# The carried state's products in four 64x64 quadrants of TensorE, with the state as the stationary operand and the outputs in two banks

## The chip, the core and the metric

The kernel runs on one core of a Trainium2 chip. Its engines are PE (TensorE, matrix products into PSUM), DVE (VectorE), ACT (ScalarE), POOL (GpSimd) and SP (SyncE, which here only issues DMAs). PEld is the loading of PE's stationary operand. The metric is the device time of one execution in microseconds (us), as the median of several runs.

## What is computed

Two stages stand in a row. The first is a linear recurrence over time for 4 batches and 8 heads of width 48, the second a two-layer network on the tokens that it gives.

```python
for t in range(S):                                   # S = 768, r, k, v, w: (4, 8, 768, 48)
    cur = np.einsum('bhd,bhe->bhde', u[None] * kt, vt)
    y[:, :, t] = np.einsum('bhd,bhde->bhe', rt, state + cur)
    state = wt[:, :, :, None] * state + np.einsum('bhd,bhe->bhde', kt, vt)
x = y.transpose(0, 2, 1, 3).reshape(B * S, H * D)    # 3072 tokens of 384
h = x @ w_in                                         # 384 x 2048
g = np.maximum(h, 0.0) + alpha * np.minimum(h, 0.0)
out = g @ w_out                                      # 2048 x 384
```

## The kernel before

**Attention.** The 768 steps are cut into 6 chunks of 128, so that with 4 batches there are 24 units q = 0 to 23 (chunk c = q // 4, batch b = q % 4). For each q, `load` brings in decays, k and r with the head's width on the partitions (`wd`, `kr`), and v (`nv`). `prep` makes running products of the decays with two scans on DVE (L367, L373) and scales k and r with them (L376, L379). `scores` (L430) multiplies k by r into two PSUM banks, DVE writes the part before the diagonal over ACT's diagonal (L435, tile `at`). `outputs` then adds three things on PE. For c > 0 the carried state acts on the scaled r (L526). The new part of the state is the transposed k times v (L479). The scores times v (L472) complete the output. Two heads lie above each other on the 128 partitions, head 2p in rows 0 to 63 and head 2p + 1 in rows 64 to 127, each 48 wide.

**The carried state.** `St[b]` holds the state of a batch, 128 x 4 x 48. `carry` scales it on POOL (L415), and ACT copies its two halves into the diagonal blocks of `Sd`, 128 x 4 x 128 with zeros elsewhere (L419, two copies). L526 then runs four products of the whole 128x128 array, one for each pair of heads. The output tile `yp` is one PSUM bank, and the new state goes to another, `up`.

**Split outputs.** The network runs in fp32r on a high and a low part of each number. `take` copies `yp` in two pieces (384 and 128 columns) to the high part on ACT (L492). The low part is the difference, on DVE (L503) from q = 6 on, before that by a product with minus the identity on PE (L497) and ACT (L501).

**Network.** Three q form a group g of 384 tokens, 8 groups in all. A step is one (g, j) with j one of 16 slices of the hidden width: 9 products L605, activation on ACT and DVE (L610, L612), the split into `gh` and `gl` (L614, L615), and two steps later 9 products L624. The weights of slice j are unpacked once from 8-byte numbers by ACT and DVE; the last of these steps is `wl` (L591, 17 instructions in all). The first three groups run j = 0 to 5 first, then j = 6 to 15, so step 28 is the first that needs the last weight slice.

**Order.** Nothing runs in the order of the code. Each piece is recorded with `op(engine, duration, function, reads, writes, due)`, and `Plan.order` places all pieces by a simulated clock with these durations, due times and free buffers. The order on each engine is what that plan gives. PSUM has three banks for the network's results and a ring of five, `bank`, for all else.

Of the kernel before, what the change touches and what calls it, by code (L numbers as in the profile page):

```python
# [20 lines left out]
P = 128  # L21
# [29 lines left out]
MODES = {("M", "R"): 0.2, ("R", "M"): 0.2, ("M", "C"): 0.1, ("C", "M"): 0.15, ("C", "R"): 0.1, ("R", "C"): 0.1}  # L51
# [162 lines left out]
def fast_path(tc, wgt, flag, dmaj, nat, u, wts, alpha, out, part):  # L214
# [12 lines left out]
    with tc.tile_pool(name="const", bufs=1) as const, tc.tile_pool(name="psum", bufs=1, space=PSUM) as psum:  # L227
# [10 lines left out]

        Sd = const.tile([P, NP, P], F32, name="Sd")
# [11 lines left out]
        St = [const.tile([P, NP, D], F32, name=f"St{b}") for b in range(B)]  # L251
# [39 lines left out]
        for o in range(2):  # L291
            op("SP", 0.4, lambda o=o: nc.sync.dma_start(
                out=u_dm[ROWS[o], :, o:o + 1], in_=u.rearrange("(p o d) -> o d p", o=2, d=D)[o].unsqueeze(2)),
               w=[("u_dm", o)], lat=0.05)
# [17 lines left out]
        op("POOL", 0.6, lambda: nc.gpsimd.memset(Sd, 0.0), w=[("Sd", 0), ("Sd", 1)])  # L312
# [44 lines left out]
        def prep(q):  # L357
# [37 lines left out]
            else:  # L395
                for i in range(2):
# [4 lines left out]
                    out=cd.ap.rearrange("p (o a) -> p a o", o=2),  # L401
                    in_=rk.ap[:, 0:HD].rearrange("p (a o d) -> p a o d", o=2, d=D), axis=AX.X, op=ALU.add), r=[rk], w=[cd])
# [52 lines left out]
        def outputs(q, nxt):  # L455


            c, b = divmod(q, B)
# [6 lines left out]
            yp = Tensor(bank)  # L465
            up = Tensor(bank) if c < NC - 1 else None
            dst = slice(0, KT)

            def pair(p, start, stop):
                for o in range(2):  # L470
                    h = 2 * p + o
                    nc.tensor.matmul(yp.ap[FULL[o], p * P:(p + 1) * P], lhsT=nv.ap[:, h * 64:(h + 1) * 64],  # L472
                                     rhs=at.ap[:, o, p, :], start=start, stop=stop)

            def state():
                for p in range(NP):
                    for o in range(2):
                        h = 2 * p + o
                        nc.tensor.matmul(up.ap[FULL[o], p * D:(p + 1) * D], lhsT=kn[:, p, FULL[o]],  # L479
                                         rhs=nv.ap[:, h * 64:h * 64 + D], start=True, stop=True)  # L480

            def take(last):


                parts = [(0, lambda i: x.ap[:, i, :, ss], x, 0.45)]
                if last:
                    parts.append((KT * P, lambda i: xr.ap[:, i, ss], xr, 0.25))

                def src(c0):
                    return pairs(yp.ap[:, 0:KT * P], P) if c0 == 0 else yp.ap[:, c0:]  # L490
                for c0, dst, key, t in parts:
                    op("ACT", t, lambda c0=c0, dst=dst: nc.scalar.copy(out=dst(0), in_=src(c0)), r=[yp], w=[(key, (s, 0))])  # L492
                if q < LO_BY_PE:

                    def rests():
                        for c0, dst, key, t in parts:
                            nc.tensor.matmul(src(c0), lhsT=minus, rhs=dst(0), start=False, stop=True, skip_group_check=True)  # L497
                    op("PE", 0.25 * len(parts), rests, r=["minus", *[(key, (s, 0)) for _, _, key, _ in parts]], w=[yp], kind="MM")
                for c0, dst, key, t in parts:
# [442 lines left out]
```

## Time and profile before

| | us |
|---|---|
| median of 3 runs | 541.84 (541.06 to 547.21) |
| profiled execution | 540.92 |
| its span, first to last instruction | 539.1 |
| PE busy in the span | 518.3 (96%) |
| DVE busy | 348.4 (65%) |
| ACT busy | 324.2 (60%) |
| POOL busy | 56.9 (11%) |

The profiled execution's own time lies 1.8 us over its span and 0.9 us under the median. An engine's busy share is an average over the span; the stages differ, and they are read one by one below. In rows, the name before `<-` is what an instruction writes, the names behind it are what it reads. A float32 product of the code shows as two PE records, an fp32r product as one.

### The profile page before, as it was taken

The page shows a single profiled execution, that of the slowest core. Times are in us where ns is not written, and L with a number is a line of the kernel's source. Part 1 is how long each engine was busy: PE and PEld are TensorE (multiplying, and loading weights), DVE is VectorE, ACT ScalarE, POOL GpSimd, SP SyncE. Part 2 cuts the span into 40 slices and gives each one's busy share as a digit, 9 for nine tenths or more (in the row PEclk, how much of TensorE's full clock was granted, in tenths as well). Part 3 has the DMA queues.
Part 4 walks back from the last instruction along what each step waited for, and adds up shares of the span by engine and source line. Part 5 has one row for each costly group of instructions (what it writes and reads, how often), then busy time and mean ns, then how long its engine had stood idle before and what let it go on. Part 6 is the DMA issues. An engine that isn't in the chain of part 4 may idle for free.

```text
span 539.1 us, 9763 instructions
## 1 busy us (share of the span) xinstructions
PE 518.3 (96%) x3733; PEld 501.0 (93%) x3733; DVE 348.4 (65%) x595; ACT 324.2 (60%) x802; POOL 56.9 (11%) x74
## 2 busy tenths in 40 slices
PE   5997989999999999999999999999999999999995
PEld 5877878989999999999999999999999999999995
DVE  5799999999995738665736566556474444333332
ACT  2677777765654346555646567668777675653332
POOL 2000514240000201210100110110000000000000
PEclk9599989999999999999999999999999999999999
DMA  8357677754623206544507344546354243021001
GB/s 303 126 179 253 249 219 255 247 170 144 191 72 102 96 12 215 160 129 142 157 28 202 115 164 127 158 169 223 120 190 141 66 155 118 11 74 42 0 2 50
DMA packets 29655, 75.14 MB, mean 139 GB/s; under 512 B 4064, under 2 KB 10912, under 8 KB 29600
## 3 DMA queue, kind: packets, MB, share of 16 engines
q1 hardware_dynamic: 29600, 74.44, 42.6%
q8 instruction: 31, 0.51, 0.4%
q14 instruction: 24, 0.20, 0.1%
HBM read 65.87 MB, written 6.49 MB: 134 GB/s over the span
## 4 chain that ended last, share of the span: by engine, by line
PE 74%; DVE 14%; DMA 5%; issue 3%; ACT 2%; SPq 1%; DVEq 0%; ACTq 0%
PE bank L605 30%; PE op L624 30%; PE bank L430 4%; DMA raw<-in_wts_dram 4%; PE bank L472 3%; PE bank L526 3%; DVE gl L615 2%; DVE raw L586 2%; DVE wd L373 2%; DVE wl L591 1%; PE bank L479 1%; DMA u_dm<-in_u_dram 1%; DVE cx L583 1%; DVE at L435 1%; PE bank L390 1%
## 5 line engine op out<-in xcount | busy, mean ns | idle before, releaser
L605 PE MATMUL bank<-x,wh 128*128 128x384 f32 x768 | 218.9, 339 | 3.2 <-ACT kn L451 1.8
L605 PEld LDWEIGHTS bank<-x,wh 128*128 128x128 f32 x768 | 140.5, 188 | 6.2 <-ACT kn L451 2.1
L610 ACT ACTIVATE pos<-bank,alpha_n 128x384 f32<-128x384 f32 x128 | 74.1, 579 | 98.6 <-PE bank L605 97.5
L624 PE MATMUL op<-wh,gl 128*128 128x384 f32 x384 | 129.5, 337 | 3.3 <-DVE gl L615 3.3
L624 PE MATMUL op<-wh,gh 128*128 128x384 f32 x384 | 129.8, 338 | 0.0
L624 PE MATMUL op<-wl,gh 128*128 128x384 f32 x384 | 129.0, 336 | 0.0
L605 PE MATMUL bank<-x,wl 128*128 128x384 f32 x384 | 128.5, 335 | 0.2 <-DVE wl L591 0.2
L612 DVE SCALAR_TENSOR_TENSOR pos<-bank,pos 128x384 f32<-128x384 f32 x128 | 70.5, 551 | 80.5 <-ACT pos L610 80.1
L615 DVE TENSOR_TENSOR gl<-pos,gh 128x384 fp32r<-128x384 f32 x128 | 74.9, 585 | 52.1 <-ACT gh L614 51.9
L614 ACT CAST gh<-pos 128x384 fp32r<-128x384 f32 x128 | 65.4, 511 | 54.2 <-DVE pos L612 54.0
L624 PEld LDWEIGHTS op<-wh,gl 128*128 128x128 f32 x384 | 72.5, 189 | 4.9 <-DVE gl L615 4.8
L624 PEld LDWEIGHTS op<-wh,gh 128*128 128x128 f32 x384 | 72.4, 189 | 0.6
L605 PEld LDWEIGHTS bank<-x,wl 128*128 128x128 f32 x384 | 72.1, 188 | 0.5 <-DVE wl L591 0.5
L624 PEld LDWEIGHTS op<-wl,gh 128*128 128x128 f32 x384 | 72.5, 189 | 0.0
L406 ACT ACTIVATE at<-ident,cd 128x128 f32<-128x128 f32 x192 | 62.8, 392 | 0.9 <-PE bank L472 0.4
L435 DVE COPY_PREDICATED at<-mask,bank 128x512 f32<-128x512 int32 x48 | 33.1, 731 | 29.3 <-PE bank L430 26.7
L415 POOL TENSOR_TENSOR St<-St,pc_all 128x192 f32<-128x192 f32 x20 | 11.5, 577 | 260.1 <-ACT pc_all L382 253.0
L367 DVE TENSOR_TENSOR_SCAN suf<-wd,low 128x520 f32<-128x520 f32 x24 | 30.4, 1267 | 3.6 <-DMA wd<-in_dmaj_dram 3.6
L373 DVE TENSOR_TENSOR_SCAN wd<-wd,low 128x520 f32<-128x520 f32 x24 | 30.8, 1282 | 0.0
L430 PE MATMUL bank<-kr 64*128 64x128 f32 x384 | 29.7, 297 | 0.8 <-DVE kr L379 0.8
L430 PEld LDWEIGHTS bank<-kr 64*128 64x128 f32 x384 | 24.9, 199 | 4.9 <-issue 3.6
L397 POOL TENSOR_TENSOR rk<-rk,u_bc 128x384 f32<-128x384 f32 x18 | 20.2, 1120 | 78.2 <-DMA rk<-in_nat_dram 56.1
(84 smaller groups left out, 497.5 us busy)
## 6 DMA issues: line engine op xcount, KB each, us to landing
raw<-in_wts_dram SPq DMA_DIRECT2D x32, 768.0 KB, 4.6
kr<-in_dmaj_dram SPq DMA_DIRECT2D x24, 512.0 KB, 3.9
rk<-in_nat_dram SPq DMA_DIRECT2D x18, 384.0 KB, 3.5
wd<-in_dmaj_dram SPq DMA_DIRECT2D x24, 260.0 KB, 2.8
raw<-in_dmaj_dram SPq DMA_DIRECT2D x12, 520.0 KB, 4.3
nv<-in_nat_dram SPq DMA_DIRECT2D x24, 256.0 KB, 4.4
out_dram<-os SPq DMA_DIRECT2D x23, 192.0 KB, 1.9
x<-x3s SPq DMA_DIRECT2D x42, 48.0 KB, 2.2
```

The costliest lines, as they stand in the source:

```text
L367: op("DVE", 1.15, lambda: nc.vector.tensor_tensor_scan(out=suf.ap[:, ::-1], data0=w.ap[:, ::-1], data1=low[:, ::-1], initial=0.0, op0=ALU. ...
L373: op("DVE", 1.15, lambda: nc.vector.tensor_tensor_scan(out=w.ap, data0=w.ap, data1=low, initial=0.0, op0=ALU.mult, op1=ALU.max), r=["low"] ...
L397: op("POOL", 1.0, lambda i=i: nc.gpsimd.tensor_tensor(out=rk.ap[:, 0:HD], in0=rk.ap[:, 0:HD], in1=u_bc if i == 0 else rk.ap[:, HD:], op=AL ...
L406: nc.scalar.activation(out=at.ap[:, o, p, :], in_=ident, func=AF.Copy, scale=cd.ap[:, o * NP + p:o * NP + p + 1])
L430: nc.tensor.matmul(sps[o].ap[:, p * P:(p + 1) * P], lhsT=kr.ap[FULL[o], 0, p, :], rhs=kr.ap[FULL[o], 1, p, :], start=True, stop=True)
L435: op("DVE", 0.62, lambda o=o: nc.vector.copy_predicated(out=at.ap[:, o], mask=mask.unsqueeze(1).broadcast_to([P, NP, P]), data=pairs(sps[o ...
L605: nc.tensor.matmul(hp.ap[:, 0:GT], lhsT=a[:, j, 0, ks], rhs=x.ap[:, xi, k, :], start=(i == 0), stop=(i == 3 * KT - 1))
L610: op("ACT", 0.5, lambda: nc.scalar.activation(out=pos.ap, in_=hp.ap[:, 0:GT], func=AF.Relu, scale=alpha_n[:, j:j + 1]), r=[hp, "alpha"], w ...
L612: op("DVE", 0.55, lambda: nc.vector.scalar_tensor_tensor(out=pos.ap, in0=hp.ap[:, 0:GT], scalar=0.0, in1=pos.ap, op0=ALU.max, op1=ALU.subt ...
L614: op("ACT", 0.41, lambda: nc.scalar.copy(out=gh.ap, in_=pos.ap), r=[pos], w=[gh])
L615: op("DVE", 0.47, lambda: nc.vector.tensor_tensor(out=gl.ap, in0=pos.ap, in1=gh.ap.bitcast(F32), op=ALU.subtract), r=[pos, gh], w=[gl], lo ...
L624: nc.tensor.matmul(ops_[s], lhsT=a.ap[:, ts], rhs=w[:, j, 1, :], start=(j == j0 and i == 0), stop=(j == j1 - 1 and i == 2))
```

## The change

`Sd` is gone. `St[b]` becomes 128 x 4 x 64 with zeros in the last 16 columns, and is itself the stationary operand. Head p now lies in rows 0 to 63 and head 4 + p in rows 64 to 127, which the host's layout, `u` and the general path follow. Each of the four products of 128x128 becomes two of 64x64: the row half is that of the head (o), the column half is p % 2. So there are eight products in the four quadrants, and row half o writes to bank `yb[o]`. The scores times v go to the same two banks, and the new state to the free columns of `yb[0]`, so `up` is gone too. `take` now has three pieces: 256 columns of `yb[0]`, and twice 128 of `yb[1]`. The plan gets other durations and mode costs.

```diff
-MODES = {("M", "R"): 0.2, ...
+MODES = {("M", "Q"): 0.1, ("Q", "M"): 0.1, ("R", "Q"): 0.1, ("C", "Q"): 0.1, ("M", "R"): 0.2, ...
-        Sd = const.tile([P, NP, P], F32, name="Sd")
-        St = [const.tile([P, NP, D], F32, name=f"St{b}") for b in range(B)]
+        St = [const.tile([P, NP, 64], F32, name=f"St{b}") for b in range(B)]
-        op("POOL", 0.6, lambda: nc.gpsimd.memset(Sd, 0.0), w=[("Sd", 0), ("Sd", 1)])
+        for b in range(B):
+            op("POOL", 0.15, lambda b=b: nc.gpsimd.memset(St[b][:, :, D:], 0.0), w=[("St", b)])
...
                 op("POOL", 0.5, lambda: nc.gpsimd.tensor_tensor(
-                    out=St[b], in0=St[b], in1=pc_all[:, q, :].unsqueeze(2).broadcast_to([P, NP, D]), op=ALU.mult),
-                   r=[("pc", q)], w=[("St", b)], lock=True)
-                for o in range(2):
-                    op("ACT", 0.25, lambda o=o: nc.scalar.copy(out=Sd[FULL[o], :, 64 * o:64 * o + D], in_=St[b][FULL[o]]),
-                       r=[("St", b)], w=[("Sd", o)])
+                    out=St[b][:, :, 0:D], in0=St[b][:, :, 0:D], in1=pc_all[:, q, :].unsqueeze(2).broadcast_to([P, NP, D]),
+                    op=ALU.mult), r=[("pc", q)], w=[("St", b)], lock=True)
...
-            yp = Tensor(bank)
-            up = Tensor(bank) if c < NC - 1 else None
+            yb = Tensor(bank), Tensor(bank)
+            up = c < NC - 1
+            open_ = set()
+            def mm(o, rows, cols, stop=False, **kw):
+                nc.tensor.matmul(yb[o].ap[rows, cols], start=(o, rows.start) not in open_, stop=stop, skip_group_check=True, **kw)
+                open_.add((o, rows.start))
+            def pair(i, stop):
+                o = i // 2
+                for e in range(2):
+                    p = 2 * (i % 2) + e
+                    h = o * NP + p
+                    mm(o, FULL[e], slice((i % 2) * P, (i % 2 + 1) * P), stop, lhsT=nv.ap[:, h * 64:(h + 1) * 64], rhs=at.ap[:, o, p, :])
+            def carried(stop):
+                for p in range(NP):
+                    for o in range(2):
+                        mm(o, FULL[p % 2], slice(p // 2 * P, (p // 2 + 1) * P), stop and p > 1, lhsT=St[b][FULL[o], p, :],
+                           rhs=kr.ap[FULL[o], 1, p, :])
             def state():
                 for p in range(NP):
                     for o in range(2):
-                        h = 2 * p + o
-                        nc.tensor.matmul(up.ap[FULL[o], p * D:(p + 1) * D], lhsT=kn[:, p, FULL[o]],
-                                         rhs=nv.ap[:, h * 64:h * 64 + D], start=True, stop=True)
+                        h = o * NP + p
+                        mm(0, FULL[o], slice(2 * P + p * D, 2 * P + (p + 1) * D), lhsT=kn[:, p, FULL[o]],
+                           rhs=nv.ap[:, h * 64:h * 64 + D])
...
-                parts = [(0, lambda i: x.ap[:, i, :, ss], x, 0.45)]
+                parts = [(0, (0, 2), lambda i: x.ap[:, i, 0:2, ss], x, 0.35), (1, (0, 1), lambda i: x.ap[:, i, 2, ss], x, 0.25)]
                 if last:
-                    parts.append((KT * P, lambda i: xr.ap[:, i, ss], xr, 0.25))
+                    parts.append((1, (1, 2), lambda i: xr.ap[:, i, ss], xr, 0.25))
...
                 def products():
                     if c > 0:
-                        for p in range(NP):
-                            nc.tensor.matmul(yp.ap[:, p * P:(p + 1) * P], lhsT=Sd[:, p, :], rhs=kr.ap[:, 1, p, :],
-                                             start=(p == 0), stop=False)
+                        carried(False)
...
-                t = 1.28 + (0.97 if c > 0 else 0) + (0.42 if up else 0) + (1.0 if sc else 0)
+                t = 1.28 + (0.55 if c > 0 else 0) + (0.42 if up else 0) + (1.0 if sc else 0)
```

Two places of the new order matter. The first is PE's row around the carried products of q = 9. Before, they stand behind the 31st network step's L605 (`Sd` is the stationary operand, `nv` is v, `kn` the transposed k, `at` the scores, `op` the network's results):

```order
L624 MATMUL op_73<-wl,gh_125 128x384
L526 MATMUL bank_78<-kr_104,Sd 128x128 x4
L479 MATMUL bank_77<-nv_109,kn 64x48 x8
L472 MATMUL bank_78<-at_116,nv_109 64x128 x8
L430 MATMUL bank_76<-kr_105 128x128
```

In the changed kernel all products of `outputs` carry the helper's line L469, and this unit stands behind the 21st step's L605:

```order
L639 MATMUL op_74<-wl,gh_122 128x384
L469 MATMUL bank_78<-kr_103,St_93 64x128
L469 MATMUL bank_76<-kr_103,St_93 64x128
L469 MATMUL bank_78<-kr_103,St_93 64x128
L469 MATMUL bank_76<-kr_103,St_93 64x128
L469 MATMUL bank_78<-kr_103,St_93 64x128
L469 MATMUL bank_76<-kr_103,St_93 64x128
L469 MATMUL bank_78<-kr_103,St_93 64x128
L469 MATMUL bank_76<-kr_103,St_93 64x128
L469 MATMUL bank_78<-nv_108,kn 64x48 x8
L469 MATMUL bank_78<-at_115,nv_108 64x128 x4
L469 MATMUL bank_76<-at_115,nv_108 64x128 x4
```

Four products have become eight, which take the two banks in turn, and the whole unit has moved ten steps forward; the other units with c > 0 look the same (20 in all, 5 ahead of step 28 before and 6 now). Of those behind, q = 10, 14 and 15 stand six to eight steps earlier, the rest about where they stood.

The second place is DVE's row around the last weight slice, `wl`. Before, the scan L367 of the prep after next stands behind the last `wl`:

```order
L591 TENSOR_TENSOR wl<-raw_100,wh 128x768
L580 TENSOR_SCALAR cx_101<-raw_99 128x768
L615 TENSOR_TENSOR gl_126<-pos_121,gh_123 128x384
L583 SCALAR_TENSOR_TENSOR cx_101<-raw_99,cx_101 128x768
L612 SCALAR_TENSOR_TENSOR pos_122<-bank_76,pos_122 128x384
L586 ISA raw_99<-raw_99,cx_101 128x768x2
L615 TENSOR_TENSOR gl_127<-pos_122,gh_124 128x384
L373 SCALAR_TENSOR_TENSOR wd_103<-wd_103,low 128x520
L591 TENSOR_TENSOR wl<-raw_99,wh 128x768
L612 SCALAR_TENSOR_TENSOR pos_121<-bank_75,pos_121 128x384
L379 TENSOR_TENSOR kr_106<-kr_106,wd_103 128x512
L367 SCALAR_TENSOR_TENSOR suf_112<-wd_102,low 128x520
```

In the changed kernel (L379, L606 and L367 are the same pieces of work) the prep's L379 and the next prep's scan L367 stand ahead of the last `wl`:

```order
L379 TENSOR_TENSOR kr_105<-kr_105,wd_102 128x512
L627 SCALAR_TENSOR_TENSOR pos_120<-bank_79,pos_120 128x384
L606 TENSOR_TENSOR wl<-raw_98,wh 128x768
L598 SCALAR_TENSOR_TENSOR cx_100<-raw_99,cx_100 128x768
L630 TENSOR_TENSOR gl_125<-pos_120,gh_122 128x384
L601 ISA raw_99<-raw_99,cx_100 128x768x2
L627 SCALAR_TENSOR_TENSOR pos_121<-bank_75,pos_121 128x384
L367 SCALAR_TENSOR_TENSOR suf_111<-wd_101,low 128x520
L606 TENSOR_TENSOR wl<-raw_99,wh 128x768
```

Counted over DVE's whole row up to the last `wl`, the changed kernel has one L379, one L367 and four L435 more, one L615 fewer, and the low parts of q = 6 to 8 in nine pieces where there were six. Up to the same point PE's row (step 28) has two more units' scores, one more unit's transposes and outputs, and six L624 fewer.

## Rows read from the trace of the kernel before

**Rows 1.** The page: the span, the busy time of PE, DVE and ACT, and the span in 40 equal slices (busy share in tenths; PEclk is the granted TensorE clock in tenths).

```profile
span 539.1 us, 9763 instructions
PE 518.3 (96%) x3733; PEld 501.0 (93%) x3733; DVE 348.4 (65%) x595; ACT 324.2 (60%) x802; POOL 56.9 (11%) x74
...
PE   5997989999999999999999999999999999999995
...
PEclk9599989999999999999999999999999999999999
```

**Rows 2.** The windows by stage: length, then the busy time (and count) of PE, PEld, DVE, ACT and POOL, the granted clock, the DMA share and GB/s.

```profile
0.00:12.00 12.00, 5.87 (x29) 5.67 (x29) 7.95 (x11) 3.15 (x11) 2.91 (x18) 0.99 0.83 287
12.00:30.00 18.00, 17.75 (x150) 16.08 (x152) 12.50 (x22) 12.23 (x40) 0.00 (x0) 0.63 0.51 186
30.00:74.00 44.00, 37.88 (x342) 33.10 (x339) 43.76 (x66) 34.06 (x91) 8.58 (x7) 0.96 0.64 222
74.00:157.50 83.50, 81.24 (x573) 78.33 (x571) 81.22 (x131) 55.71 (x121) 19.70 (x19) 1.00 0.58 187
157.50:467.20 309.70, 309.40 (x2268) 302.29 (x2268) 178.38 (x321) 190.75 (x483) 25.67 (x30) 1.00 0.41 131
467.20:533.40 66.20, 66.13 (x382) 65.53 (x380) 24.55 (x48) 27.80 (x57) 0.00 (x0) 1.00 0.09 26
```

**Rows 3.** The windows of L526 alone (each product is two records).

```profile
30.00:157.50 127.50, 5.31 (x40) 5.11 (x40) 0.99 0.60 199
157.50:467.20 309.70, 15.78 (x120) 15.52 (x120) 1.00 0.41 131
```

**Rows 4.** The chain of waits around 157 us: start, length, what.

```profile
155.38 1.15 DVE wd L373
156.53 0.86 DVE wl L591
157.39 0.04 issue
157.44 1.68 PE bank L605 x8
```

**Rows 5.** PE's timeline around one unit with c > 0: start, length, line, shapes (stationary, then moving), count.

```profile
209.70 0.33 PE L624 MATMUL op<-wh,gl 128*128 128x384 f32 x1
209.87 0.34 PE L624 MATMUL op<-wl,gh 128*128 128x384 f32 x1
210.05 1.05 PE L526 MATMUL bank<-kr,Sd 128*128 128x128 f32 x8
211.03 0.67 PE L479 MATMUL bank<-nv,kn 128*64 128x48 f32 x16
211.53 1.06 PE L472 MATMUL bank<-at,nv 128*64 128x128 f32 x16
212.52 1.16 PE L430 MATMUL bank<-kr 64*128 64x128 f32 x16
213.62 0.44 PE L624 MATMUL op<-wh,gh 128*128 128x384 f32 x1
213.90 0.34 PE L624 MATMUL op<-wh,gl 128*128 128x384 f32 x1
214.07 0.34 PE L624 MATMUL op<-wl,gh 128*128 128x384 f32 x1
```

**Rows 6.** The same unit in narrow cuts of the timeline, each from another window: 211.04 to 211.05, 211.60 to 211.64, 211.64 to 211.70, 212.31 to 212.325 and 212.50 to 212.53. A row counts the records that run in its window.

```profile
210.83 0.28 PE L526 MATMUL bank<-kr,Sd 128*128 128x128 f32 x1
...
211.53 0.29 PE L472 MATMUL bank<-at,nv 128*64 128x128 f32 x2
...
211.53 0.41 PE L472 MATMUL bank<-at,nv 128*64 128x128 f32 x4
...
212.10 0.50 PE L472 MATMUL bank<-at,nv 128*64 128x128 f32 x6
...
212.31 0.28 PE L472 MATMUL bank<-at,nv 128*64 128x128 f32 x2
```

**Rows 7.** PE's timeline where a full-array product is followed by L430 alone, at 58 us.

```profile
58.22 0.34 PE L605 MATMUL bank<-x,wh 128*128 128x384 f32 x1
58.49 1.16 PE L430 MATMUL bank<-kr 64*128 64x128 f32 x16
59.58 0.45 PE L624 MATMUL op<-wh,gh 128*128 128x384 f32 x1
59.87 0.34 PE L624 MATMUL op<-wh,gl 128*128 128x384 f32 x1
```

**Rows 8.** Groups of instructions by line and shape: count, busy us, mean ns of one, and the idle time before them.

```profile
L435 DVE COPY_PREDICATED at<-mask,bank 128x512 f32<-128x512 int32 x48 | 33.1, 731 | 29.3 <-PE bank L430 26.7 <-ACT at L406 2.7
...
L367 DVE TENSOR_TENSOR_SCAN suf<-wd,low 128x520 f32<-128x520 f32 x24 | 30.4, 1267 | 3.6 <-DMA wd<-in_dmaj_dram 3.6
L379 DVE TENSOR_TENSOR kr<-kr,wd 128x512 f32<-128x512 f32 x24 | 16.4, 683 | 0.0
...
L503 DVE TENSOR_TENSOR x<-bank,x 128x384 fp32r<-128x384 f32 x18 | 9.8, 545 | 1.3 <-ACT x3s L492 1.3
...
L503 DVE TENSOR_TENSOR x3s<-bank,x3s 128x128 fp32r<-128x128 f32 x18 | 5.1, 281 | 0.0
```

**Rows 9.** The same view: the copies into `Sd`, and the high parts on ACT.

```profile
L419 ACT COPY Sd<-St 64x192 f32<-64x192 f32 x40 | 14.0, 349 | 2.2 <-PE bank L526 2.0
...
L492 ACT CAST x<-bank 128x384 fp32r<-128x384 f32 x24 | 11.3, 472 | 10.4 <-PE bank L472 10.4
...
L492 ACT CAST x3s<-bank 128x128 fp32r<-128x128 f32 x21 | 5.7, 269 | 0.0
```

**Rows 10.** PE's timeline where it starts again after a wait; in brackets the idle time and what ended it.

```profile
50.41 0.44 PE L605 MATMUL bank<-x,wh 128*128 128x384 f32 x1 [1.85 <-ACT kn L451]
...
70.02 0.69 PE L624 MATMUL op<-wh,gl 128*128 128x384 f32 x1 [1.35 <-DVE gl L615]
```

**Rows 11.** The windows around that second wait.

```profile
70.00:75.00 5.00, 4.99 (x21) 4.70 (x21) 4.89 (x9) 3.99 (x10) 0.74 (x2) 0.68 0.58 168
```

More of the change, by code (lines that the diff above doesn't have):

```diff
@@ L400, in prep @@
                 op("DVE", 0.47, lambda: nc.vector.tensor_reduce(
-                    out=cd.ap.rearrange("p (o a) -> p a o", o=2),
-                    in_=rk.ap[:, 0:HD].rearrange("p (a o d) -> p a o d", o=2, d=D), axis=AX.X, op=ALU.add), r=[rk], w=[cd])
+                    out=cd.ap, in_=pairs(rk.ap[:, 0:HD], D), axis=AX.X, op=ALU.add), r=[rk], w=[cd])
             for o, ps in ((o, range(i, i + 2)) for o in range(2) for i in (0, 2)):
@@ L486, in take, with src @@
                 if last:
-                    parts.append((KT * P, lambda i: xr.ap[:, i, ss], xr, 0.25))
[L489 to L492, printed above, removed]
+                    parts.append((1, (1, 2), lambda i: xr.ap[:, i, ss], xr, 0.25))
+                def src(o, i):
+                    return pairs(yb[0].ap[:, 0:2 * P], P) if o == 0 else yb[o].ap[:, i[0] * P:i[1] * P]
@@ L493, in take @@
+                for o, i, dst, key, t in parts:
+                    op("ACT", t, lambda o=o, i=i, dst=dst: nc.scalar.copy(out=dst(0), in_=src(o, i)), r=[yb[o]], w=[(key, (s, 0, o))])
                 if q < LO_BY_PE:
                     def rests():
-                        for c0, dst, key, t in parts:
-                            nc.tensor.matmul(src(c0), lhsT=minus, rhs=dst(0), start=False, stop=True, skip_group_check=True)
-                    op("PE", 0.25 * len(parts), rests, r=["minus", *[(key, (s, 0)) for _, _, key, _ in parts]], w=[yp], kind="MM")
@@ L499, in take @@
-                for c0, dst, key, t in parts:
+                        for o, i, dst, key, t in parts:
+                            nc.tensor.matmul(src(o, i), lhsT=minus, rhs=dst(0), start=False, stop=True, skip_group_check=True)
+                    op("PE", 0.2 * len(parts), rests, r=["minus", *[(key, (s, 0, o)) for o, _, _, key, _ in parts]], w=yb, kind="MM")
+                for o, i, dst, key, t in parts:
                     if q < LO_BY_PE:
-                        op("ACT", t, lambda c0=c0, dst=dst: nc.scalar.copy(out=dst(1), in_=src(c0)), r=[yp], w=[(key, (s, 1))])
+                        op("ACT", t, lambda o=o, i=i, dst=dst: nc.scalar.copy(out=dst(1), in_=src(o, i)), r=[yb[o]], w=[(key, (s, 1, o))])
@@ L513, in products @@
                 def products():
-                    for p in range(KT):
-                        nc.tensor.matmul(yp.ap[:, p * P:(p + 1) * P], lhsT=spread()[:, p, :], rhs=t3(s), start=(p == 0), stop=False)
-                    for p in range(KT):
-                        pair(p, False, p == KT - 1)
-                op("PE", 1.9, products, r=[sp, x3, (at, 0), (at, 1), nv], w=[yp], kind="MC", due=due_att[q] + 2.0)
-                op("PE", 0.5, state, r=["kn", nv], w=[up], kind="CC", due=due_att[q] + 10.0)
+                    for e in range(2):
+                        open_.discard((1, FULL[e].start))
@@ new lines, in products @@
+                    for i in range(KT):
+                        nc.tensor.matmul(yb[i // 2].ap[:, (i % 2) * P:(i % 2 + 1) * P], lhsT=spread()[:, i, :], rhs=t3(s),
+                                         start=(i % 2 == 0), stop=False, skip_group_check=True)
+                    open_.update((o, FULL[e].start) for o in range(2) for e in range(2))
+                    for i in range(KT):
+                        pair(i, i > 0)
+                op("PE", 1.9, products, r=[sp, x3, (at, 0), (at, 1), nv], w=yb, kind="MC", due=due_att[q] + 2.0)
```

69 lines of the change are left out of this document (34 added, 35 removed).

## The prediction

> **What bounds the kernel now.** I read the page first: PE is busy for 518.3 of 539.1 us, DVE for 348.4, ACT for 324.2, and after the first quarter PE's line shows full slices [rows 1]. Then I read the windows by stage [rows 2]. From 157.5 to 467.2 us PE is idle for 0.3 us, from there to 533.4 for 0.1. In this stretch whatever PE no longer does comes off the end, and what other engines do is free: DVE works for 178 of 310 us there, ACT for 191. Ahead of 157.5 us PE is idle for 6.1, 0.2, 6.1 and 2.3 us, and DVE is busy for 43.8 of 44.0 and 81.2 of 83.5 us. That front is ruled by both, and its last wait is PE's for the last weight slice: DVE ends a scan and `wl` at 157.39, PE goes on at 157.44 [rows 4]. The end is therefore T, the moment at which the last weight slice is unpacked, plus all PE work that the order leaves behind it.
>
> **Term 1: the carried products themselves.** Now L526 takes eight records from 210.05 to 211.03, that is 0.98 us per unit, in one step with the full-array products ahead of it (209.87 to 210.05 is the usual 0.18) [rows 5]. There are 40 records ahead of 157.5 us and 120 behind, so 5 and 15 units [rows 3]. Afterwards there are 16 records in four quadrants. No row shows four quadrants, so I build the price from the two-tile forms. In L472 two column halves run side by side: two records run in the cut from 211.60, four in that from 211.64, so they start in pairs; pairs start at 212.10 and 212.31 with one between, 0.105 us for a step [rows 6]. L430 shows the same for two row halves: 16 records in 1.10 us with the change of form at its start [rows 5]. If all four quadrants run side by side, 16 records are four steps, 0.42 us.
>
> To this come changes of form. L526 stands in the full-array form, as the network does, so today the unit changes form when L479 begins: the last L526 starts at 210.83 [rows 6], L479 at 211.03 [rows 5], 0.20 instead of a step of 0.11, so 0.09 more. From the full array to L430 it is 58.22 to 58.49, 0.27 instead of 0.17, so 0.10 [rows 7]; from L472 to L430 212.31 to 212.52, again 0.10 more than a step [rows 5, 6]. The changed unit goes in with one such change and out to L479 with another, where there was only the latter. Going into L430 and out of it costs about a further 0.1 for a stationary operand of 128 columns that isn't loaded ahead (213.62 to 213.90 is 0.28, not 0.17 [rows 5]). With 64 columns, I take 0.04 for it, between nothing and 0.10. Sum: 0.10 + 0.04 + 0.42 + 0.10 = 0.66 us against 0.98, **0.32 us saved per unit** (0.26 to 0.36 by the bounds). By the new order 14 units stand behind step 28, which is where the last weight slice is first used: 14 x 0.32 = **4.5 us off**.
>
> On how many quadrants run together, a row and a rule differ. L472's pairs both hold all 128 rows of the array, and its 16 loads of 64 columns fit in the same 0.99 us as its records [rows 5], so loads there run beside products of the same rows. The Trainium skill, "TensorE: Matmul & The Clock Gate", section "Part 3: Packing small matmuls — row/col tiling", says that a load overlaps running products only where the row group differs, and the new order returns to the same row group with every second product. By that rule the change loses; I carry it as a rival. The same section reports 16 small tiles at 10.6 times the speed of one, which speaks for four at once; no row here shows either.
>
> **Term 2: the front.** The new order moves more attention ahead of the last weight slice. On DVE this is one L379, one L367, four L435, and three more pieces of low part, less one L615. With the mean durations [rows 8] that is 0.68 + 1.27 + 4 x 0.73 = 4.9 us, and 0.45 for the low parts (a slope of 264 ns over 256 columns puts the 256-column piece at 0.41 us, so 0.41 + 0.28 + 0.28 replace 0.55 + 0.28, 0.15 for each of three units). Less one L615 of about the duration of the 384-column low part, 0.55, this is 4.8 us. Such durations overlap by about 0.1 in DVE's queue (the chain counts 1.15 us for a scan that lasts 1.28 [rows 4, 8]), so I take **T later by 4.2 us**, with 3.5 and 4.8 as ends.
>
> The same pieces of PE work then no longer stand behind T. They are, at today's prices: scores that stand alone, 1.09 us and 0.10 + 0.12 for the changes of form [rows 7], 1.3; a whole unit from 210.05 to 213.62 with 0.1 for the way out, 3.7 [rows 5]; transposes, four records more, which at the scores' 0.07 a record and 0.1 for a change of form are 0.4; less six L624 of 0.17, 1.0. Together **4.4 us off** behind T. So the front nets -0.2 us: it is a shift of work, not a gain. The 0.32 us saved in the front's own six units turns into idle time of PE, because DVE rules T.
>
> **Terms that cost nothing.** ACT loses 40 copies of 0.35 us and gains about 0.17 per unit for the third piece of the high part [rows 9]; both lie under PE, since ACT is busy for six tenths of the PE-bound stretch. DVE's 0.15 us per unit are hidden there too (it would cost them if DVE, at 58% in this stretch, had no slack). The new-state products and the scores' products keep their forms. Two banks instead of one are held until the low parts are taken; a unit with the next scores takes four of five as before, and the last four units, which took three, now take four. PE is idle for 0.3 us in this stretch, so the fifth bank has sufficed. The carried products wait for POOL's scaling alone and no longer for two ACT copies behind it. SP issues the same DMAs.
>
> **Sum.** 540.92 - 4.5 - 0.2 = 536.2 for the profiled execution. The timed runs lie at 541.06 and 541.84, 0.1 to 0.9 above it, so I add 0.4 and predict **536.6 us**, 1.0% less. A measurement of this kernel can tell some 2% from no change, so this counts as "within".
>
> **Rival A: only two quadrants run side by side** (the change doesn't do what it says). 16 records are eight steps, 0.84 + 0.24 = 1.08 us instead of 0.98, and 14 units lose 1.4 us: 536.6 + 14 x 0.42 = 542.5. For it: each float32 product is two records on the same quadrant, and no row shows more than two records starting together [rows 6]. Against it: the pairs prove that PE starts the other tile's record ahead of the second record of the first, since with strict order the first and the last record of L472 would stand alone. Chance 0.14.
>
> **Rival B: slower, by loads that wait for their rows.** If the load of a quadrant waits until products in the same row half are through, a pair of row halves costs a step and a load: 0.105 + 0.06 (L479's 16 loads of 64 columns fill 0.50 us in pairs, 0.06 a pair [rows 5]). Eight such pairs are 1.3 us, with 0.24 for the changes of form 1.6, 0.6 more than today. 14 x 0.6 = 8.4 us more, which with the front's -0.2 and the 0.4 for the runs gives 549.5. It decides from 0.98 us per unit on. L472's rate speaks against it. This is the rule of the Trainium skill named above; the trace disagrees for column halves, and shows nothing on quadrants. Chance 0.06.
>
> **Rival C: the front loses.** DVE's order in the first 70 us changes too, with more preps ahead of the early weight slices. PE waits there already, once for 1.85 and once for 1.35 us [rows 10], and after the second of these the granted clock of a 5 us window is 0.68, that is 1.2 GHz instead of 2.4 for two thirds of it [rows 11]; from 12 to 30 us it is 0.63 [rows 2]. One more such wait of 2 us, with two thirds of 5 us at half clock behind it, costs 2 + 1.7: 536.6 + 3.7 = 540.3. For it: nothing in the new order fills such a wait on purpose. Against it: PE and DVE are both nearly full from 74 us on, and what PE loses ahead of T it partly would have waited anyway. Chance 0.16. The opposite is part of the forecast's own range: DVE is idle for 5.5 us from 12 to 30 us [rows 2], and the preps moved forward may use this; T is then some 2 us earlier and the time 534.6, with 0.36 us per unit 534.
>
> **How the numbers follow.** Four quadrants at once with the front as computed: 0.64, predicted 536.6, with the bounds of the terms 533 to 539. Rival A 0.14 at 542.5, B 0.06 at 549.5, C 0.16 at 540.3. The range from 532.8 to 542.2 holds nearly all of the forecast and of C and some of A; it leaves out B and most of A. Faster by over 2% needs 531.0, which takes both a full gain in all 20 units and a front better by 3 us: 0.02. Slower by over 2% needs 552.7: rival B with a bad front, 0.02. Within: 0.96.
>
> **What the profile will show.** Right: in the PE-bound stretch the next product (L479's, now under L469) begins 0.6 to 0.7 us after the first carried record, whose starts come four at a time; PE's idle time behind the last weight slice stays under 1 us; `wl` ends for the last time near 161 us; PE's idle time in the front grows by 1 to 2 us. Rival A shows pairs and 1.1 us, B pairs with gaps and 1.6 us, C a longer wait of PE ahead of 100 us with a lower granted clock behind it. I would be wrong in the sum if PE waited for a bank behind a unit, or if the front's order made DVE itself wait for PE.

## The result, and the profile after

The changed kernel takes **544.74 us** (median of 20 runs, 542.15 to 547.38), the kernel before 541.24 beside it: ratio **1.0077 (1.0059 to 1.0094)**, 0.8% slower, where 1% faster was forecast. The profiled execution took 543.57 us. In what follows a time is the median of all runs, while a ratio leaves out single slow runs and need not be the quotient of two medians.

The page of the changed kernel, the lines that answer to [rows 1]: PE is busy as long as before, and the clock line has more low digits in the first seven slices.

```profile
span 541.8 us, 10119 instructions
...
PE 518.2 (96%) x3899; PEld 495.3 (91%) x3899; DVE 356.7 (66%) x613; ACT 314.0 (58%) x792; POOL 58.4 (11%) x77
...
PEclk8579798999999999999999999999999999999999
```

Its windows by stage, columns as in [rows 2]:

```profile
0.00:12.00 12.00, 5.73 (x30) 5.52 (x31) 7.95 (x11) 3.15 (x11) 2.80 (x21) 0.95 0.82 288
12.00:30.00 18.00, 17.64 (x127) 16.14 (x127) 13.39 (x22) 11.97 (x41) 0.00 (x0) 0.56 0.47 159
30.00:74.00 44.00, 36.28 (x349) 31.83 (x350) 40.74 (x59) 28.49 (x83) 10.16 (x9) 0.84 0.58 195
74.00:157.50 83.50, 80.43 (x647) 74.66 (x644) 81.70 (x129) 55.30 (x130) 17.85 (x17) 0.98 0.64 207
157.50:467.20 309.70, 309.70 (x2342) 299.96 (x2342) 186.95 (x344) 185.62 (x470) 27.63 (x30) 1.00 0.41 131
```

A granted clock of 0.84 in a stretch of 44 us means that 0.16 x 2 x 44 = 14.1 us of it ran at 1.2 GHz instead of 2.4; this time is called half clock below. Summed over the stages it is 34 us, against 17 in [rows 2]. A steady unit (PE's timeline, as [rows 5]; L469 now holds all three kinds of products):

```profile
255.25 0.34 PE L639 MATMUL op<-wl,gh 128*128 128x384 f32 x1
255.52 0.67 PE L469 MATMUL bank<-kr,St 64*64 64x128 f32 x16
256.12 0.67 PE L469 MATMUL bank<-nv,kn 128*64 128x48 f32 x16
256.62 1.06 PE L469 MATMUL bank<-at,nv 128*64 128x128 f32 x16
257.61 1.16 PE L426 MATMUL bank<-kr 64*128 64x128 f32 x16
258.70 0.44 PE L639 MATMUL op<-wh,gh 128*128 128x384 f32 x1
```

From the first carried record to the next product it is 0.60 us (0.98 before), and 0.27 instead of 0.17 on the way in, so 0.70 for 0.98.

Step 28 begins at 168.6 us, where it began at 156.9 before. From there to PE's end it takes 367.0 us instead of 376.4. So 9.4 us are won behind step 28 and 11.7 lost ahead of it. The rows are step 28's first product and PE's last one, before:

```profile
156.89 0.34 PE L605 MATMUL bank<-x,wh 128*128 128x384 f32 x1
...
532.99 0.34 PE L624 MATMUL op<-wl,gh 128*128 128x384 f32 x1
```

and after, with the last `wl` on DVE ahead of them:

```profile
167.38 0.93 DVE L606 TENSOR_TENSOR wl<-raw,wh 128x768 fp32r<-128x768 f32 x1
...
168.65 0.33 PE L620 MATMUL bank<-x,wh 128*128 128x384 f32 x1
...
535.26 0.34 PE L639 MATMUL op<-wl,gh 128*128 128x384 f32 x1
```

The front is all that stands ahead of step 28. Its waits, to set beside those in [rows 10] (in brackets the idle time and what ended it):

```profile
45.61 1.02 PE L390 MATMUL bank<-u_dm,rk 128*128 128x2 f32 x8 [1.70 <-DVE rk L363]
53.85 0.40 PE L469 MATMUL bank<-kr,St 64*64 64x128 f32 x2 [1.68 <-ACT kn L447]
56.01 1.12 PE L469 MATMUL bank<-kr,St 64*64 64x128 f32 x14 [1.76 <-DVE pos L627]
```

A fourth, of 1.42 us, ends at 32.9. The last of the three stands inside a unit. Two quadrant records ran; then the unit's second bank was still held by a result of the network's first products, until DVE had read `pos` from it. The window from 55 to 62 us, which begins within this wait, has a granted clock of 0.51, and that from 34 to 42 us has 0.57.

### The profile page after: what moved, and what is told of

It reads as the page before. It is cut to its first block, busy times and chain, and to the rows that moved or that the text cites. A ratio compares the mean times of both kernels' runs of the same rounds, so it can differ in the third digit from the quotient of the medians.

```text
span 541.8 us, 10119 instructions
## 1 busy us (share of the span) xinstructions
PE 518.2 (96%) x3899; PEld 495.3 (91%) x3899; DVE 356.7 (66%) x613; ACT 314.0 (58%) x792; POOL 58.4 (11%) x77
## 4 chain that ended last, share of the span: by engine, by line
PE 75%; DVE 13%; DMA 7%; issue 2%; ACT 1%; SPq 1%; DVEq 0%; ACTq 0%
PE bank L620 31%; PE op L639 31%; PE bank L469 6%; DMA raw<-in_wts_dram 4%; PE bank L426 4%; DVE raw L601 2%; DVE gl L630 2%; DVE wl L606 2%; DVE cx L598 1%; DVE pos L627 1%; DMA u_dm<-in_u_dram 1%; DVE cx L595 1%; PE bank L390 1%; PE bank L445 1%; DVE suf L367 1%
## 5 line engine op out<-in xcount | busy, mean ns | idle before, releaser
L630 DVE TENSOR_TENSOR gl<-pos,gh 128x384 fp32r<-128x384 f32 x128 | 77.1, 604 | 46.9 <-ACT gh L629 46.5
L367 DVE TENSOR_TENSOR_SCAN suf<-wd,low 128x520 f32<-128x520 f32 x24 | 31.2, 1300 | 3.7 <-POOL ones L314 3.7
L426 PE MATMUL bank<-kr 64*128 64x128 f32 x384 | 30.9, 305 | 0.0
L469 PE MATMUL bank<-at,nv 128*64 128x128 f32 x384 | 28.8, 295 | 0.1
```

What stands on the lines that cost most here:

```text
L367: op("DVE", 1.15, lambda: nc.vector.tensor_tensor_scan(out=suf.ap[:, ::-1], data0=w.ap[:, ::-1], data1=low[:, ::-1], initial=0.0, op0=ALU. ...
L426: nc.tensor.matmul(sps[o].ap[:, p * P:(p + 1) * P], lhsT=kr.ap[FULL[o], 0, p, :], rhs=kr.ap[FULL[o], 1, p, :], start=True, stop=True)
L469: nc.tensor.matmul(yb[o].ap[rows, cols], start=(o, rows.start) not in open_, stop=stop, skip_group_check=True, **kw)
L630: op("DVE", 0.47, lambda: nc.vector.tensor_tensor(out=gl.ap, in0=pos.ap, in1=gh.ap.bitcast(F32), op=ALU.subtract), r=[pos, gh], w=[gl], lo ...
```

## The experiments

A ratio is to the kernel before on the same chip, with its 95% interval; places in time and half clock are those of the profiled execution. An edit of the plan's input changes the order too, since the plan is made anew. Two theories stood at first: **F**, the new order gives the front away; **S**, something in the new structure does.

**Orders exchanged.** Either kernel was given the other's order on every engine, as a list:

```
-                    heapq.heappush(ready[e], (ops[n].due, n))
+                    heapq.heappush(ready[e], (ops[n].prio, n))   # prio: place in the other kernel's order
```

> The changed kernel, whole, but its pieces are placed by a list that holds the order of the kernel before (a piece that does not exist there follows its neighbour; three pieces late in the program are let past). Theory F, the front: the 3.5 us lost come from the new order ahead of the last weight slice, which lets PE wait longer and brings it to half clock for 34 us instead of 17. Then this run has the front of the kernel before (last weight slice near 157 to 160 us, some 17 us at half clock) and keeps the 0.29 us per unit behind it: 535 to 538 us, ratio 0.987 to 0.995. Theory S, the structure: the loss comes from the two shared banks and the third piece of high and low parts, wherever they stand. Then it stays at 543 to 546 us.

548.44 us, 1.0158 (1.0131 to 1.0184), slower than either theory said, with 27 us of half clock. Behind step 28 it takes 371.3 us, 5.1 less than before for 15 units: the quadrants alone, 0.34 a unit, or 0.31 without the 0.5 us that PE idled there before and no longer does. But PE now waits 4.07 us at a place where the kernel before, in this order, waits for nothing:

```profile
37.22 1.87 PE L487 MATMUL bank<-u_dm,rk 128*128 128x2 f32 x8 [4.07 <-ACT x L609]
```

It waits for a bank which comes free only with ACT's copies out of it.

> The kernel before, whole, but placed by a list that holds the order of the changed kernel (the two copies into Sd follow POOL's scaling). Theory F: it takes over the bad front, 30 us or more at half clock and the last weight slice near 165 to 169 us, and has no quadrants: 547 to 551 us. Theory S: it stays at 540 to 542 us.

552.68 us, 1.0249 (1.0211 to 1.0288), 27 us of half clock. Each order is bad for the other kernel, so neither F nor S alone stands. This suggests that an order fits only the banks that it was planned for.

**More made-up products at the start**, in both kernels (products that nobody reads, which keep PE at work until its first inputs land):

```
-MADE = 12
+MADE = 24
```

> The changed kernel with MADE = 24 instead of 12 products at PE's start that nobody reads, so that PE works on through its wait for u_dm (8.5 to 11.6 us); the plan's order is untouched. If PE's wait there is what brings on the 17 us at half clock from 10.8 us on, that stretch goes and PE gets through its first units up to 8 us earlier: 536 to 540 us. If the front is ruled by DVE, PE then only waits later: 543 to 545 us.

541.81 us, 1.0023 (0.9986 to 1.006); half clock is 20.5 us instead of 34.

> The kernel before with MADE = 24. Its 13.7 us at half clock from 11.8 us on go in the same way. If PE's clock rules the front, 535 to 538 us; if DVE rules it, as I had argued from its nearly full windows, 540 to 542 us.

539.13 us, 0.9981 (0.9953 to 1.0008); half clock is 3.4 us instead of 17. The changed kernel gains some 3 us and stays 2.7 behind; the gain of 1.2 us in the kernel before isn't clear of the noise.

**The banks.** In the four first units nothing is carried, but the change gives them two banks for outputs, and their new state lies in the first of them. So the state waits behind the outputs and the outputs' copies wait for the state. That this costs the front is **Theory B**; **Rival N** puts the loss down to the numbers of the plan. One edit keeps the old arrangement in these units (its core):

```
-            yb = Tensor(bank), Tensor(bank)
+            yb = (Tensor(bank),) * 2 if c == 0 else (Tensor(bank), Tensor(bank))
+            ub = Tensor(bank) if c == 0 else yb[0]          # the state's bank
```

> The changed kernel, but the four first units (chunk 0, no carried state, so no quadrants) keep their outputs in one bank and their state in a bank of its own, as the kernel before does; the quadrants and two banks stay in the units that carry a state. Theory B (two banks held until the low parts are taken, and a state that must wait behind the products that share its bank, make TensorE wait early in the front, and its clock falls): step 28 comes 8 to 12 us earlier than in the changed kernel (157 to 161 us instead of 168.6), behind it the 367.0 us of the changed kernel stay, 532 to 537 us. Rival N (the plan's new durations for the quadrant units move the order, the banks don't matter): the front stays lost, 541 to 546 us.

539.91 us, 0.9996 (0.9954 to 1.0037): 4.8 us better than the change, not the 8 to 12 expected. Step 9 comes at 92.6 us (101.0 in the changed kernel, 93.0 before) and half clock is 13.7 us, but step 28 still comes at 165.3.

The opposite, on the kernel before: the state's bank is held with the outputs' (the core of the edit).

```
-   op("PE", 1.9, products, ..., w=[yp], ...)        op("ACT", t, ..., r=[yp], ...)
+   op("PE", 1.9, products, ..., w=[yp, up], ...)    op("ACT", t, ..., r=[yp, up], ...)
```

> The kernel before, full array everywhere, with one thing of the change: a unit's two banks are held together. The state's bank comes free only when the outputs' low parts have been taken, and the outputs' first copy waits for the unit's own state too. Theory B (the banks alone cost the front): half clock over 25 us or more ahead of step 28, step 28 at 163 to 170 us, 546 to 553 us. Rival N (numbers of the plan): as the kernel before, 540 to 543 us.

544.17 us, 1.0054 (1.0024 to 1.0085), half clock 20.5 us. Holding banks costs some 3 us by itself, less than Theory B's 546 to 553 us said.

In between: the changed kernel with a third bank for the state in those units, the outputs still in two (the core of the edit).

```
+            ub = Tensor(bank) if c == 0 else yb[0]
-                op("PE", 0.5, own_state, r=["kn", nv], w=[yb[0]], kind="CC", due=due_att[q] + 10.0)
+                op("PE", 0.5, own_state, r=["kn", nv], w=[ub], kind="CC", due=due_att[q] + 10.0)
```

> The changed kernel, with one edit: in the four first units the state is written to a third bank of its own, not to the rest of the outputs' first bank; the outputs keep their two banks. Theory S (the state that shares a bank, waits behind the outputs and holds their copies up is what breaks the front): step 1 at 36 to 41 us instead of 48.3, half clock under 22 us, step 28 at 158 to 163 us, 534 to 539 us. Rival H (two banks for the outputs are enough to break it): step 1 at 46 us or later, 542 to 546 us.

539.06 us, 0.9968 (0.9936 to 1.0); step 1 comes at 37.5 us (48.3 in the changed kernel), half clock is 24 us, and step 28 comes at 162.0. The changed kernel missed the forecast by 8.1 us. This edit alone takes 5.7 of them back, so that is what the state in the outputs' bank costs, by the waits, by the order that the plan makes of it and by the clock together.

**The plan's number** for a carried unit, put back in the changed kernel (with kind "M" for "Q"), and the other way round, alone, in the kernel before:

```
-                t = 1.28 + (0.55 if c > 0 else 0) + (0.42 if up else 0) + (1.0 if sc else 0)
+                t = 1.28 + (0.97 if c > 0 else 0) + (0.42 if up else 0) + (1.0 if sc else 0)
```

> The changed kernel, planned with the kernel before's duration and kind for a unit that carries a state (0.97 us and full array instead of 0.55 us and quadrants); what runs is the same work. Theory B: the front stays lost, half clock over 25 us or more, 541 to 547 us. Rival N: the front comes back, step 28 near 157 us, 533 to 537 us.

545.03 us, 1.0083 (1.0047 to 1.0119), half clock 34 us: the number isn't the cause.

> The kernel before, with one number of the plan changed: a unit that carries a state counts 0.42 us less (0.55 instead of 0.97), as in the changed kernel; what runs is the same work in the order that this gives. Theory D (the number alone moves one more attention unit ahead of step 28, where it costs nothing in the end): step 28 at 160 to 165 us, behind it about 372 us, 540 to 544 us. Rival: the order hardly moves, step 28 near 157 us, 540 to 542 us.

540.37 us, 1.0003 (0.9983 to 1.0024). Behind step 28 it takes 373.0 us instead of 376.4: one unit more stands ahead of it, and as forecast this is worth nothing at the end. Step 28 came at 158.4 and not at 160 to 165; half clock fell to 10 us in this order.

**The clock by itself.** The changed kernel in its own order, with products that nobody reads laid into its waits. **Theory C** says that the fall of the clock behind the waits is the larger part of the loss, **Rival O** that the order and the waits themselves are:

```
+FILL = {("sums", 1): 10, ("sums", 5): 5, ("sums", 6): 6, ("Q", 1): 6}
             for o in order:
+                if o.eng == "PE":
+                    fill(FILL.get(...))   # so many 128x128 products into an unused part of ops_[2]
                 o.fn()
```

> The changed kernel in its own order, with made-up products (128x128 by 128x128, read by nobody) laid into four of its waits ahead of the products that wait: 10 into the wait of 3.06 us at 11.6 us, 5 into the 1.42 us at 32.9, 6 into the 1.70 us at 45.6, 6 into the 1.68 us at 53.8. They take away what the clock falls after, and add no work where they fit into the wait. Theory C (the clock's fall behind the waits is the larger part of the lost front): half clock under 15 us instead of 34, step 28 at 158 to 162 us instead of 168.6, 535 to 539 us. Rival O (the order and the waits themselves cost it, the clock only goes with them): step 28 stays over 164 us, 541 to 545 us.

538.6 us, 0.9962 (0.993 to 0.9994): **6.1 us off by added work**. Half clock is 13.7 us instead of 34. The windows, to set beside those above:

```profile
12.00:30.00 18.00, 17.54 (x159) 15.92 (x158) 15.32 (x25) 14.66 (x52) 0.00 (x0) 0.72 0.59 204
30.00:74.00 44.00, 38.28 (x389) 33.05 (x388) 43.90 (x62) 29.27 (x86) 16.55 (x12) 1.00 0.64 221
```

The time is Theory C's. Step 28 at 165.4 us is Rival O's: PE now waits 3.5 us at 85 us for a DMA that it waited 0.5 us for in the changed kernel. This profiled execution took 540.36 us, 1.8 more than the median, so the places in time show less of the gain than the medians do.

**Both causes away, in both kernels.** The third bank with filled waits, less and more, and the kernel before with 22 such products in three of its waits (by the place of the operation on PE that they stand ahead of):

```
+FILL = {2: 8, 13: 4, 22: 3, 33: 2, 47: 6, 61: 5}     # third bank
+FILL = {2: 14, 13: 4, 22: 3, 33: 8, 47: 6, 61: 5}    # third bank, more
+FILL = {2: 10, 35: 7, 51: 5}                         # the kernel before
```

> The kernel with quadrants and a third bank for the first units' state, in its own order, with made-up products in its waits on TensorE: 8 into the 2.20 us at 11.3 us, 4 into the 1.21 us at 28.5, 3 into the 1.14 us at 37.1, 2 into the 0.68 us at 49.8, 6 into the 1.89 us at 68.6, 5 into the 1.62 us at 83.3. If the forecast's saving behind step 28 is real and only the front hid it (bank and clock): half clock under 12 us, step 28 at 156 to 160 us, 533 to 537 us. If the front loses for another reason: 538 to 540 us.

536.7 us, 0.9936 (0.9911 to 0.9961); half clock is still 20 us.

> The kernel before in its own order, with made-up products in three of its waits: 10 into the 2.93 us at 11.9 us, 7 into the 1.85 us at 50.4, 5 into the 1.35 us at 70.0. It says what the filling is worth without the quadrants. Half clock falls from 17 us to under 6 us; step 28 at 152 to 155 us; 537 to 540 us. If the filling of the changed kernel had gained by anything but the clock: no gain here, 541 us.

536.99 us, 0.9952 (0.9926 to 0.9977), no half clock; step 28 comes at 152.5.

> The kernel with quadrants, the third bank and filled waits, with more made-up products in the two waits that were left of it: 14 instead of 8 into the wait for the bias column at 11.3 us, 8 instead of 2 into the wait at 49.9 us, behind which half-clock stretches of 13.7 and 6.8 us came. If the clock is all that is left of the loss: half clock under 5 us, step 28 at 156 to 159 us, 530 to 534 us, 3 to 6 us under the kernel before with its waits filled (536.99). If the quadrant kernel's front loses for a further reason: 535 to 538 us with the clock up.

537.37 us, 0.9924 (0.9894 to 0.9953), no half clock. Third bank and filling together take 7.4 to 8.0 us off the changed kernel, less than the sum of 5.7 and 6.1: their gains overlap, since the third bank already lowers half clock. Against the kernel before with filled waits there is no gain clear of the noise: its ratio is 0.9952, on another chip, and the intervals overlap. The page of the kernel before with filled waits, and its group of the filling products (count, busy us, mean ns):

```profile
span 535.4 us, 9855 instructions
...
PE 516.8 (97%) x3779; PEld 499.2 (93%) x3779; DVE 350.1 (65%) x595; ACT 323.9 (60%) x802; POOL 57.8 (11%) x74
...
PEclk9999999999999999999999999999999999999998
```

```profile
L660 PE MATMUL op<-os 128*128 128x128 f32 x46 | 6.1, 284 | 0.0
```

The same of the quadrants with the third bank and the larger filling:

```profile
span 535.7 us, 10272 instructions
...
PE 515.3 (96%) x3981; PEld 491.5 (92%) x3981; DVE 352.4 (66%) x613; ACT 313.0 (58%) x792; POOL 63.0 (12%) x77
...
PEclk9999999999999999999999999999999999999998
```

```profile
L680 PE MATMUL op<-os 128*128 128x128 f32 x82 | 10.6, 279 | 0.0
```

PE's own work is 516.8 - 6.1 = 510.7 us in the one and 515.3 - 10.6 = 504.7 in the other: the quadrants save 6.0 us of it (5.7 where a filling product's overlap with its neighbours counts as work). PE ends at 529.0 us in both, so it waits, idle or filled, for 18.3 us in the one and 24.3 in the other. Step 28 moved from 152.5 to 160.5 us, and what stands behind it from 376.5 to 368.5 us:

```profile
152.51 0.34 PE L606 MATMUL bank<-x,wh 128*128 128x384 f32 x1
```

```profile
160.54 0.34 PE L626 MATMUL bank<-x,wh 128*128 128x384 f32 x1
```

**The old arrangement of banks in the first units**, with the clock kept up: with 24 products at the start, with the third group's units planned a step later too, and with filled waits.

```
-PLACE = {0: (-1, -1, -1), 1: (1, 3, 4), 2: (7, 8, 9)}
+PLACE = {0: (-1, -1, -1), 1: (1, 3, 4), 2: (8, 9, 10)}    # the second only
+FILL = {2: 13, 51: 5, 57: 4}                              # the third only
```

> As the kernel with one bank in the first units, with 24 made-up products at the start instead of 12. Theory B and the clock's part in it: half clock under 12 us in all, step 28 at 153 to 157 us, 529 to 533 us, under both kernels. Rival N: 539 to 543 us, as the changed kernel with 24.

537.21 us, 0.9908 (0.9873 to 0.9944), though step 28 stands at 163.4 and half clock is 13.7 us. The kernel before with the same 24 products stood at 0.9981 (0.9953 to 1.0008), so here the timed runs show a gain of 0.7% over the kernel before with the clock helped alike. The two were timed on two chips, though, and their profiled executions are equal (537.62 and 537.64 us).

> As the kernel with one bank in the first units and 24 made-up products, with the third group's units due one step later each (8, 9, 10 instead of 7, 8, 9). If the order between step 9 and step 28 still costs the 3 us of waits that the kernel with one bank has there more than the changed kernel: 534 to 537 us. If not: 537 to 541 us.

538.85 us, 0.9967 (0.9936 to 0.9997), slower than the 534 to 537 hoped for: waits of 4.4 and 2.6 us stand in other places.

> The kernel with one bank in the first units, in its own order, with made-up products in three waits: 13 into the 1.96 us at 11.2 us, 5 into the 1.23 us at 69.4, 4 into the 1.05 us at 75.3. Its half clock was 13.7 us. If the clock is what is left: half clock under 4 us, step 28 at 159 to 162 us, 533 to 536 us. If not, 537 to 540 us.

536.33 us, 0.9929 (0.9902 to 0.9956). Step 9 comes at 87.0 us, 1.3 ahead of the filled kernel before. Some 1.0 of this is only order, since six records of the network's second products fewer stand ahead of it (54 against 60, 0.17 each). From there to step 28 PE idles 3.4 us instead of 1.1, and half clock comes back for 3.4 us. This version and the one with 24 products are 0.7 to 0.9% faster than the kernel before; half of that or more the kernel before gets by filled waits alone (0.9952).

## Why the prediction was wrong

**Term 1 was right.** With the way in, 0.66 us per unit were forecast and 0.70 measured. The saving was to be 0.32 (0.26 to 0.36); it is 0.28 to 0.29 by a unit's rows, and 0.31 to 0.34 with the order held. Over all units 6.0 us of PE's work went; 14 x 0.32 and six units in the front were 6.4.

**Rivals A and B are out.** Four quadrants start together. Narrow cuts of the unit above, at 255.61, 255.71 and 255.81 us, count 4, 8 and 12 records, with a step of 0.10 to 0.11 us from each four to the next:

```profile
255.52 0.34 PE L469 MATMUL bank<-kr,St 64*64 64x128 f32 x4
...
255.52 0.45 PE L469 MATMUL bank<-kr,St 64*64 64x128 f32 x8
...
255.52 0.56 PE L469 MATMUL bank<-kr,St 64*64 64x128 f32 x12
```

The rule weighed for rival B (the Trainium skill, "TensorE: Matmul & The Clock Gate", "Part 3: Packing small matmuls — row/col tiling": loads pass running products only in another row group) would have given 1.6 us here. The trace disagrees: every second product returns to the same rows, and the 16 records take 0.60 us.

**Behind step 28 the sum held:** 4.5 + 4.4 = 8.9 us were forecast and 9.4 measured, of which 0.5 is idle time that PE had there before and has no longer. That the other 8.9 match to the tenth is partly luck: at 0.28 to 0.29 us a unit, 14 units give 4.0, and so the moved work some 4.9 instead of 4.4.

**Term 2 failed, by the clock.** T was to come 4.2 us later and came 11.7 later (11 by `wl`, which ends at 168.3 and not near 161). PE's end is its work, its idle time, and what half clock adds to the work. Taking the work from the two kernels with filled waits, 510.7 and 504.7, the rest of PE's busy time is put down to half clock:

| us | work | added by half clock | idle | PE ends |
|---|---|---|---|---|
| before | 510.7 | 518.3 - 510.7 = 7.6 | 15.0 | 533.3 |
| after | 504.7 | 518.2 - 504.7 = 13.5 | 17.4 | 535.6 |
| change | -6.0 | +5.9 | +2.4 | +2.3 |

The idle time grew by 2.4 us, about as forecast (1 to 2, the 1.9 saved in the front's units). The clock's 5.9 stood in no term of the sum. They are a difference, not a direct measurement, but two other readings come near. Filling the waits took half clock from 34 to 13.7 us and the median down by 6.1. And of the 12 runs of the kernel before with filled waits, three had a mean granted clock of 0.985 and took 539.6 to 540.9 us, while nine had 0.994 to 0.998 and took 535.2 to 538.6. That is some 12 us of half clock for 3.5 us between the groups' medians; at this price the 17 us more of the changed kernel would be an estimated 5 us.

Against 536.2 the profiled execution is 7.4 us long: 5.9 for the clock, 0.5 for idle time, 0.4 for work, 0.4 behind PE's end, and 0.2 that the front was to gain.

**Rival C was what happened**, and too cheap. It priced one more wait of 2 us with one stretch of half clock behind it, 3.7 us, by [rows 11]. In truth the waits of the whole front changed places: four of 1.4 to 1.8 us stand in place of one of 1.85 and one of 1.35, and half clock went from 17 to 34 us. Its chance of 0.16 looks low in hindsight: the front's order on PE was new from the first outputs on, at 21 us, and nothing in it held the clock up.

**The step that let it in** stands under "Terms that cost nothing": "the fifth bank has sufficed". That was read from the stretch behind T only. The front has units without scores, and there the state's products moved into the outputs' bank; this wasn't costed at all. A third bank for four units takes 5.7 us of the loss back. The forecast had named PE waiting for a bank behind a unit as a sign of error; the wait at 56.01 is such a wait, though inside a unit.

**That DVE rules T** was wrong for the changed kernel: PE has no wait over 0.3 us between 101 us and its end, so it sets step 28 itself.

**What stays open** is how much of the 6.0 us of work comes off the end once the clock is at full speed in both. In the profiled executions with third bank and filling none of it does: step 28 lies 8.0 us later, not 4.2, and PE waits 6.0 us more in all. The timed runs leave room for 0.3% there (0.9924 against 0.9952, not clear of the noise) and show 0.7% with 24 products and the old banks. Whether the larger filling is part of what is lost, or whether DVE's and ACT's chain sets the front whatever PE saves, wasn't separated. The version with one bank and filled waits, in which PE idles 2.3 us more between step 9 and 28 than in the filled kernel before, speaks for the order there.

## What to carry to other kernels

Price a faster product only in the stretch where PE never waits, and list separately every buffer that the edit holds longer or shares, in each stretch of the program and not in the steady one alone. Where waits of PE change places, price the clock behind each of them from a row, since here it cost more (5.9 us) than the added waits themselves (2.4). Laying products that nobody reads into the waits, with the order untouched, is a one-run test of whether a loss is the clock's; here it was worth 1.1% in the changed kernel and 0.5% in the one before.

## What the runs showed of the hardware

**Half clock followed waits of 1.4 to 2.2 us, but not each of them.** In the changed kernel it came from 34.6 to 41.5 us (granted clock 0.51), behind the wait of 1.42 us that ended at 32.9; behind the 1.70 us that ended at 45.6 the clock stayed at 1.00 until 55. The wait alone doesn't decide it: with 24 products at the start, nearly the same first rows ran at full clock in the kernel before and fell to half at 14.7 us in the version with one bank, whose last wait ahead of it was 0.16 us, in front of the 128x2 products (L390).

**DVE can be slowed beside POOL.** Ahead of the wait at 56.01 POOL works on L397 from 51.04 to 52.77 and from 52.85 to 54.67. DVE's scan, wholly beside it, takes 2.04 us (1.23 in most other places), and its unpacking step, half beside it, 1.70 (0.95). A `pos`, which reads a bank, keeps its time beside POOL: at 72.11 it took 0.53 us while L397 ran from 71.75 to 72.77.

```profile
51.83 2.04 DVE L367 TENSOR_TENSOR_SCAN suf<-wd,low 128x520 f32<-128x520 f32 x1
53.79 1.70 DVE L601 CUSTOM_DVE_ANT_0 raw<-raw,cx 128x1536 uint16<-128x1536 uint16 x1
...
72.11 0.53 DVE L627 SCALAR_TENSOR_TENSOR pos<-bank,pos 128x384 f32<-128x384 f32 x1
```

Not every scan beside POOL lost as much: the one at 241.01 took 1.34 us, and there L397 itself took 1.95 us instead of some 1.0.

The Trainium skill, "GPSIMD Engine Reference", "1. Specifications", says that GpSimd shares its SBUF interface with VectorE and contends with DVE instructions of two SBUF inputs; the trace agrees for the two lengthened steps here, each of which reads two tiles, neither in a bank. By these durations some 1.6 us of PE's wait at 56.01 hung on it, an estimate; no run without POOL's work there was made.
